# Two gated long convolutions: intermediate layouts in which PSUM copies write short contiguous runs

## The chip, the cores and the metric

The kernel runs on one core of a Trainium2 chip. The metric is the device time of one execution in microseconds (us). The engines are called as in the profile: PE (TensorE, matmuls), PEld (its weight loads), DVE (VectorE), ACT (ScalarE), POOL (GpSimd) and SP (SyncE, which here only issues DMAs).

## The reference, cut to what matters

Input x has 2048 time steps of 448 channels in bf16. Branch A is a state-space convolution: its kernel is a sum over 256 complex modes per channel. Branch B multiplies x by a convolution of a gated, shifted product of k and v with a kernel that is given. A sigmoid gate mixes the two.

```python
# A: kernel from modes, then a causal convolution of length 2048
P = exp(logdA[:, :, None] * arange(L));  K = einsum("dn,dnl,dn->dl", C, P, dB).real
a = irfft(rfft(pad(u)) * rfft(pad(K)))[:L] + u * Dskip
# B: 4-tap shift of k, product with v, causal convolution with ssm_k
kv = shift(k, shift_k) * v
b  = x * (irfft(rfft(pad(kv)) * rfft(pad(ssm_k)))[:L] + kv * ssm_D)
g  = sigmoid((x * gate_w).sum(-1, keepdims=True))
return g * a + (1 - g) * b
```

## The kernel before, in words

Time is split as 32 x 64 (a, b) and the channels as 4 groups of 112. A tile of data has the partition (group, a) and the free dimensions b (64) and channel (112). The 112 channels are worked on in two halves H of 56, each seen as 2 x 28: the pair index h and the index w (NW = 28).

Each convolution is done by transforms that are written as matmuls.

- `fft` has two stages. The first, on line L212, takes for each w one 128 x 128 block of data as the stationary operand and 256 columns (real and imaginary part r, 32 frequencies k, 4 groups g). Four such results fill one PSUM tile `ps_c` (128 x 1024, f32), and `evac` copies it to the tile `zs` in SBUF as bf16; seven copies make up one `zs`. In the second stage (L223 to L226) each of the 32 values of k takes four matmuls of 112 columns from `zs`. Four values of k fill one PSUM tile `ps_2` (2 parts of 448), which `evac` copies to `dst`, called X for data and K for a convolution kernel. Eight such copies make up one X or K.
- `products` multiplies X and K on DVE into T and, in place, X (L257, L259, L260).
- `inverse` has two stages as well. The first (L240) takes four matmuls of 256 columns for each w, four w to a PSUM tile `ps_a`, and `evac` copies it to U (seven copies). The second (L248) takes two matmuls of 56 columns for each of the 64 values of b, 16 values of b to a PSUM tile `ps_b`. DVE consumes that tile directly: `epilogue_B` (L639) multiplies it into the tile ug, and `epilogue_A` multiplies it by the gate (L646) and adds it to ug (L649).
- `KGen.block` makes an eighth of branch A's kernel. DVE builds powers of the modes in the tile `kg_T` (about 60 instructions: L294 to L332), and PE sums them in 224 small matmuls (L342) into `ps_k`, which `evac` copies to a slice of the tile S. The tile `kg_T` has one buffer, so a block can begin only when the matmuls of the one before have read it. Three small copies on ACT (L284, L285, L311) start a block. After four blocks `KGen.gather` (L377) spreads S into the tile KT.

`evac` is one line, `nc.scalar.copy(dst, src)` on L508; so all these copies stand under that line in the profile, on ACT, and are told apart by their tiles.

The program runs eight transforms and four inverses: K and X of branch B for the first half and its inverse, the same for the second half, then branch A. The eight generator blocks stand between them. The language's scheduler fixes the order of the instructions on each engine when the kernel is built, and semaphores carry the dependences, so each engine works through its own list in order. Large tiles (zs, X, K, T, U, kv, uu, ...) share a pool of five buffers, and PSUM tiles of the transforms share three.

In the layouts before the change, `zs` is [r, k, g, w], so one copy, which goes through w and then through (r, k, g), writes consecutive elements 28 elements apart. `U` is [w, h, r, b], which one copy fills in order; the second stage then reads 56 columns that lie 128 or 256 elements apart. S is [b, h, v], and the copy goes through b innermost, writing 56 elements apart. The gate's multiplication of u (L607) reads the factor `og`, one value for each b, with the step 0 along the 112 channels.

## Time and profile before

| | us |
|---|---|
| median of 3 runs | 691.45 (689.78 to 693.69) |
| profiled execution, its own time | 694.0 |
| profiled execution, its span | 692.2 |
| PE busy (PEld busy) | 285.0 (253.0) |
| DVE busy | 302.7 |
| ACT busy | 413.0 |
| POOL busy | 10.6 |

Over the span the granted TensorE clock has a mean of 0.696 of full speed. The rows of the profile show an instruction's line, engine, operation, the tile that it writes and those it reads, the shapes, the number of instructions, and busy time, mean duration and the idle time of the engine just before them with what ended it. "Chain" is the chain of work that ended last, followed back from the last instruction to whatever released each step. Line numbers are those of the kernel before, unless a row is said to be of the changed kernel, where most lines stand two or three further down.

### The profile page before, as it was taken

To read this page: it belongs to the slowest core of one execution; us is meant where nothing else is said; L and a number is where in the kernel's file an instruction comes from. 1 tells how busy PE (TensorE), PEld (TensorE's weight loads), DVE (VectorE), ACT (ScalarE), POOL (GpSimd) and SP (SyncE) were. 2 spreads that over 40 slices of the span, in tenths; PEclk is the share of its full clock that TensorE was granted. 3 is DMA by queue.
4 is the path that set the end of the run, shared out by engine and by line. 5 is a ranking of instruction groups with operands and counts; after the bars stand their busy time and mean duration, and the time that the engine had idled before them with its cause. 6 is when DMAs were issued, how large, how long until landed. Compare 5 with 4: busy or idle time off the path is not lost.

```text
span 692.2 us, 9722 instructions
## 1 busy us (share of the span) xinstructions
PE 285.0 (41%) x4272; PEld 253.0 (37%) x4272; DVE 302.7 (44%) x554; ACT 413.0 (60%) x238; POOL 10.6 (2%) x122
## 2 busy tenths in 40 slices
PE   1100123103844951216154197353126983531694
PEld 1000113102843951106153197342124971521584
DVE  5378431892297958009105975046019330000403
ACT  0556999309861440898966053990983539899340
POOL 4000000000000000000000000000000000000000
PEclk9999999655566955556567595576656955665685
DMA  9976410017101141000100181000000000000005
GB/s 186 121 112 166 110 29 1 0 25 113 59 0 47 22 80 43 4 0 1 45 2 1 46 109 39 8 2 2 0 0 1 3 1 0 1 0 1 1 1 106
DMA packets 77602, 25.74 MB, mean 37 GB/s; under 512 B 73592, under 2 KB 76536, under 8 KB 77560
## 3 DMA queue, kind: packets, MB, share of 16 engines
q1 hardware_dynamic: 59372, 20.72, 15.0%
q10 hardware_dynamic: 18188, 4.40, 4.0%
q8 instruction: 33, 0.54, 0.3%
q14 instruction: 9, 0.07, 0.0%
HBM read 17.09 MB, written 8.03 MB: 36 GB/s over the span
## 4 chain that ended last, share of the span: by engine, by line
ACT 42%; PE 27%; DVE 21%; issue 4%; ACTq 2%; POOL 1%; DMA 1%; POOLq 0%; SPq 0%
ACT zs L508 32%; PE ps_a L240 7%; PE ps_b L248 7%; DVE kg_P L294 5%; PE ps_k L342 4%; PE ps_gate L602 2%; DVE kv L590 2%; DVE T L257 2%; DVE kg_T L301 2%; DVE kg_T L302 2%; PE ps L223 1%; ACT X L508 1%; DVE kvt L589 1%; PE ps L225 1%; PE ps L224 1%
## 5 line engine op out<-in xcount | busy, mean ns | idle before, releaser
L508 ACT CAST zs<-ps_c 128x1024 bf16<-128x1024 f32 x56 | 248.0, 4831 | 53.6 <-PE ps_c L212 53.6
L294 DVE TENSOR_TENSOR kg_P<-kg_T,kg_E 128x896 bf16<-128x896 bf16 (+2 forms) x104 | 73.5, 745 | 98.2 <-ACT kg_T L285 98.2
L223 PE MATMUL ps<-zs,s_C 128*128 128x112 bf16 x256 | 61.7, 249 | 84.2 <-ACT zs L508 84.2
L508 ACT CAST S<-ps_k 128x448 bf16<-128x448 f32 x8 | 18.2, 2275 | 103.0 <-PE ps_k L342 103.0
L240 PE MATMUL ps_a<-sa_r,T 128*128 128x256 bf16 x224 | 46.3, 293 | 44.2 <-DVE T L257 30.7
L224 PEld LDWEIGHTS <-s_S 128*128 128x128 bf16 x256 | 30.4, 119 | 86.7 <-issue 86.7
L224 PE MATMUL ps<-zs,s_S 128*128 128x112 bf16 x256 | 61.8, 250 | 0.0
L225 PE MATMUL ps<-zs,s_N 128*128 128x112 bf16 x256 | 61.6, 249 | 0.0
L226 PE MATMUL ps<-zs,s_C 128*128 128x112 bf16 x256 | 61.4, 249 | 0.0
L248 PE MATMUL ps_b<-U,sb_G 128*128 128x56 bf16 x512 | 50.8, 275 | 3.9 <-ACT U L508 3.9
L248 PEld LDWEIGHTS <-sb_G 128*128 128x128 bf16 x512 | 49.9, 122 | 4.8 <-issue 4.8
L257 DVE TENSOR_TENSOR T<-X,K 128x7168 bf16<-128x7168 bf16 x4 | 15.6, 3888 | 82.3 <-ACT K L508 81.8
L508 ACT CAST U<-ps_a 128x1024 bf16<-128x1024 f32 x28 | 28.5, 1025 | 35.9 <-PE ps_a L240 35.8
L212 PE MATMUL ps_c<-Wc,sk 128*128 128x256 bf16 x56 | 12.7, 385 | 89.6 <-DVE sk L566 59.6
L240 PE MATMUL ps_a<-sa_r,X 128*128 128x256 bf16 x224 | 45.3, 288 | 3.4 <-DVE X L260 2.1
L240 PEld LDWEIGHTS <-T 128*128 128x128 bf16 x224 | 29.2, 147 | 46.1 <-DVE T L257 44.8
L212 PEld LDWEIGHTS <-sk 128*128 128x128 bf16 x56 | 7.1, 130 | 94.5 <-DVE sk L566 60.1
L342 PE MATMUL ps_k<-kg_T 128*32 128x32 bf16 x1792 | 31.1, 241 | 21.3 <-DVE kg_T L301 12.1
L342 PEld LDWEIGHTS <-kg_T 128*32 128x32 bf16 x1792 | 29.0, 148 | 23.9 <-DVE kg_T L301 12.3
L212 PE MATMUL ps_c<-Wc,kv 128*128 128x256 bf16 x56 | 12.7, 381 | 59.7 <-DVE kv L591 32.2
L307 DVE TENSOR_TENSOR kg_T<-kg_E 128x112 bf16<-128x112 bf16 x8 | 1.7, 217 | 76.1 <-PE ps_k L342 71.5
L508 ACT CAST X<-ps 128x896 bf16<-128x896 f32 x32 | 27.8, 930 | 11.0 <-PE ps L226 7.9
(139 smaller groups left out, 585.9 us busy)
## 6 DMA issues: line engine op xcount, KB each, us to landing
kg_E<-ed SPq DMA_DIRECT2D x8, 756.0 KB, 4.4
ed<-ks_E SPq DMA_DIRECT2D x11, 448.0 KB, 3.4
uu<-in_A_u_dram SPq DMA_DIRECT2D x6, 448.0 KB, 8.8
skraw<-in_B_ssm_k_dram SPq DMA_DIRECT2D x16, 112.0 KB, 4.8
ed<-ks_mag SPq DMA_DIRECT2D x5, 224.0 KB, 4.1
kt<-in_B_k_dram ACTq DMA_DIRECT2D x2, 448.0 KB, 12.8
kt<-in_B_k_dram SPq DMA_DIRECT2D x2, 448.0 KB, 12.1
vt<-in_B_v_dram ACTq DMA_DIRECT2D x2, 448.0 KB, 15.2
```

The costliest lines, as they stand in the source:

```text
L212: nc.tensor.matmul(pt[:, i, :], lhsT=cols(4 * j + i), rhs=W[:], start=True, stop=True)
L223: nc.tensor.matmul(re, lhsT=c, rhs=zr, start=True, stop=False)
L224: nc.tensor.matmul(re, lhsT=s, rhs=zi, start=False, stop=True)
L225: nc.tensor.matmul(im, lhsT=n, rhs=zr, start=True, stop=False)
L226: nc.tensor.matmul(im, lhsT=c, rhs=zi, start=False, stop=True)
L240: nc.tensor.matmul(pt[:, i, :], lhsT=lhsT, rhs=r, start=(n == 0), stop=(n == 3))
L248: nc.tensor.matmul(o, lhsT=G[:, b, r].rearrange("p g a -> p (g a)"), rhs=U[:, :, :, r, b].rearrange("p w h -> p h w"), start=(r == 0), sto ...
L257: V.tensor_tensor(out=T[:].rearrange("p r k c -> p (r k c)"), in0=X[:].rearrange("p r k c -> p (r k c)"), in1=K[:].rearrange("p r k c -> p ...
L294: V.tensor_tensor(out=P4[:, :, i * m:(i + 1) * m].rearrange("p v n c m -> p v (n c) m"), in0=T[:, lo:lo + m].rearrange("p n c m -> p (n c) ...
L301: V.tensor_tensor(out=T[:, dst:dst + n, 0], in0=P4[:, 0, 0:n, 0], in1=P4[:, 1, 0:n, 1], op=ALU.subtract)
L342: nc.tensor.matmul(pt[32 * g:32 * g + 32, hw, :].rearrange("p (i j) -> p i j", i=2), lhsT=T[:, 0:32, c, m], rhs=rhs, start=(hf == 0 and c ...
L508: nc.scalar.copy(dst, src)
```

## The change

Five layouts change, and with them the access patterns of the instructions that write or read them; the matmuls and their number stay.

- `zs` becomes [r, k, w, g]. One copy now goes through (r, k), then 4 values of w, then 4 groups, and writes 16 elements in a row; from PSUM it reads four f32 in a row and then jumps by 256. The second stage's 112 columns become (w, g).
- The copy into X or K undoes that: it reads PSUM with the step 4, and it is issued once for each of the two parts, so 128 copies of 448 elements take the place of 64 of 896. X and K keep their layout.
- `U` becomes [r, b, w, h], with the columns of the three R tables ordered (c, h) to match. One copy writes 8 elements in a row and reads two f32 in a row, then jumps by 256. The 56 columns of the last stage's matmuls are now contiguous, and the result in `ps_b` comes as (w, h); the epilogues read it with the step 2 to keep ug as it was.
- The copy into S goes through the channels innermost: it writes 7 elements in a row and reads PSUM with the step 32.
- `og` holds each value twice, and L607 is written over pairs of channels.

```diff
--- before.py
+++ after.py
@@ -129,9 +129,9 @@
         nc.scalar.activation(v[:], low16(ph[:].rearrange("p i b -> p (i b)")), ACT.Sin, scale=PHASE)
         out = []
         for nm, lo, sg in (("1", 0, 1.0), ("2", 0, -1.0), ("3", 128, 1.0)):
-            R = self.pool.tile([P, 2, 128], bf16, name="sa_r" + nm)
+            R = self.pool.tile([P, 128, 2], bf16, name="sa_r" + nm)
             for h in range(2):
-                nc.vector.tensor_scalar(out=R[:, h, :], in0=v[:, lo:lo + 128], scalar1=mask[:, h:h + 1], scalar2=sg,
+                nc.vector.tensor_scalar(out=R[:, :, h], in0=v[:, lo:lo + 128], scalar1=mask[:, h:h + 1], scalar2=sg,
                                         op0=ALU.mult, op1=ALU.mult)
             out.append(R)
         return out
@@ -204,32 +204,34 @@
 
 def fft(nc, psum, pool, W, C2, cols, dst, evac):
     C, S, N = C2
-    zs = pool.tile([P, 2, 32, 4, NW], bf16, name="zs", tag="big")
-    zw = zs[:].rearrange("p r k g w -> p w (r k g)")
+    zs = pool.tile([P, 2, 32, NW, 4], bf16, name="zs", tag="big")
+    zw = zs[:].rearrange("p r k w g -> p (r k) w g")
     for j in range(NW // 4):
         pt = psum.tile([P, 4, 256], f32, name="ps_c", tag="ps")
         for i in range(4):
             nc.tensor.matmul(pt[:, i, :], lhsT=cols(4 * j + i), rhs=W[:], start=True, stop=True)
-        evac(zw[:, 4 * j:4 * j + 4, :], pt[:])
+        evac(zw[:, :, 4 * j:4 * j + 4, :], pt[:].rearrange("p i (rk g) -> p rk i g", g=4))
     for kk in range(8):
         pt = psum.tile([P, 2, 512], f32, name="ps_2", tag="ps")
         for i in range(4):
             k = 4 * kk + i
             o = i * 112
-            zr = zs[:, 0, k].rearrange("p g w -> p (g w)")
-            zi = zs[:, 1, k].rearrange("p g w -> p (g w)")
+            zr = zs[:, 0, k].rearrange("p w g -> p (w g)")
+            zi = zs[:, 1, k].rearrange("p w g -> p (w g)")
             re, im = pt[:, 0, o:o + 112], pt[:, 1, o:o + 112]
             c, s, n = (t[:, k].rearrange("p h s -> p (h s)") for t in (C, S, N))
             nc.tensor.matmul(re, lhsT=c, rhs=zr, start=True, stop=False)
             nc.tensor.matmul(re, lhsT=s, rhs=zi, start=False, stop=True)
             nc.tensor.matmul(im, lhsT=n, rhs=zr, start=True, stop=False)
             nc.tensor.matmul(im, lhsT=c, rhs=zi, start=False, stop=True)
-        evac(dst[:, :, 4 * kk:4 * kk + 4, :].rearrange("p r k c -> p r (k c)"), pt[:, :, 0:448])
+        for r in range(2):
+            evac(dst[:, r, 4 * kk:4 * kk + 4, :].rearrange("p k (g w) -> p k g w", g=4),
+                 pt[:, r, 0:448].rearrange("p (k w g) -> p k g w", k=4, g=4))
 
 
 def inverse(nc, psum, pool, R, G, T, X, evac, consume):
-    R1, R2, R3 = (r[:].rearrange("p h c -> p (h c)") for r in R)
-    U = pool.tile([P, NW, 2, 2, 64], bf16, name="U", tag="big")
+    R1, R2, R3 = (r[:].rearrange("p c h -> p (c h)") for r in R)
+    U = pool.tile([P, 2, 64, NW, 2], bf16, name="U", tag="big")
     prods = ((T[:, 0], R1), (T[:, 1], R2), (X[:, 0], R3), (X[:, 1], R3))
     for j in range(NW // 4):
         pt = psum.tile([P, 4, 256], f32, name="ps_a", tag="ps")
@@ -238,15 +240,15 @@
             for n, (t, r) in enumerate(prods):
                 lhsT = t.rearrange("p k (g w) -> p (k g) w", w=NW)[:, :, w]
                 nc.tensor.matmul(pt[:, i, :], lhsT=lhsT, rhs=r, start=(n == 0), stop=(n == 3))
-        evac(U[:, 4 * j:4 * j + 4].rearrange("p w h r b -> p w (h r b)"), pt[:])
+        evac(U[:, :, :, 4 * j:4 * j + 4].rearrange("p r b w h -> p (r b) w h"), pt[:].rearrange("p i (rb h) -> p rb i h", h=2))
     for b0 in range(0, 64, 16):
         pt = psum.tile([P, 2, 512], f32, name="ps_b", tag="ps")
         for i in range(16):
             b = b0 + i
-            o = pt[:, i // 8, (i % 8) * 56:(i % 8) * 56 + 56].rearrange("p (h w) -> p h w", h=2)
+            o = pt[:, i // 8, (i % 8) * 56:(i % 8) * 56 + 56]
             for r in range(2):
                 nc.tensor.matmul(o, lhsT=G[:, b, r].rearrange("p g a -> p (g a)"),
-                                 rhs=U[:, :, :, r, b].rearrange("p w h -> p h w"), start=(r == 0), stop=(r == 1))
+                                 rhs=U[:, r, b].rearrange("p w h -> p (w h)"), start=(r == 0), stop=(r == 1))
         consume(b0, pt)
 
 
@@ -342,7 +344,7 @@
                         nc.tensor.matmul(pt[32 * g:32 * g + 32, hw, :].rearrange("p (i j) -> p i j", i=2),
                                          lhsT=T[:, 0:32, c, m], rhs=rhs, start=(hf == 0 and c == 0), stop=(hf == 1 and c == 1),
                                          tile_position=(0, 32 * g))
-        evac(S[:].rearrange("p b (h v) -> p h v b", h=2)[:, :, v0:v0 + CW, :], pt[:].rearrange("p (h w) b -> p h w b", h=2))
+        evac(S[:].rearrange("p b (h v) -> p b h v", h=2)[:, :, :, v0:v0 + CW], pt[:].rearrange("p (h w) b -> p b h w", h=2))
 
     def gather(self, cons, S, KT, evac):
         nc = self.nc
@@ -602,9 +604,10 @@
             nc.tensor.matmul(pg[:], lhsT=ones[:], rhs=ug[:, :, l], start=(l == 0), stop=(l == 111))
         gt = wp.tile([P, 64], f32, name="gt")
         sg = nc.scalar.activation(gt[:], pg[:], ACT.Sigmoid)
-        og = wp.tile([P, 64], bf16, name="og")
-        V.tensor_scalar(out=og[:], in0=gt[:], scalar1=-1.0, scalar2=1.0, op0=ALU.mult, op1=ALU.add)
-        V.tensor_tensor(out=ug[:], in0=uu[:], in1=og[:].unsqueeze(2).to_broadcast([P, 64, 112]), op=ALU.mult)
+        og = wp.tile([P, 64, 2], bf16, name="og")
+        V.tensor_scalar(out=og[:], in0=gt[:].unsqueeze(2).to_broadcast([P, 64, 2]), scalar1=-1.0, scalar2=1.0, op0=ALU.mult, op1=ALU.add)
+        pairs = lambda t: t[:].rearrange("p b (n t) -> p b n t", t=2)
+        V.tensor_tensor(out=pairs(ug), in0=pairs(uu), in1=og[:].unsqueeze(2).to_broadcast([P, 64, 56, 2]), op=ALU.mult)
 
         R = cons.stage_a(cons.field("sA", 0, 63), cons.onehot("mhA", 2, cons.field("hA", 6, 1)))
         G = cons.stage_b(cons.field("kB", 2, 31, 4.0, 1.0), cons.onehot("mgB", 4, cons.field("gB", 0, 3), 1.0 / 2048))
@@ -636,17 +639,17 @@
         def consume(b0, pt):
             for i in range(2):
                 o = ug[:, b0 + 8 * i:b0 + 8 * i + 8, :].rearrange("p b (h v) -> p b h v", h=2)[:, :, :, H * NW:(H + 1) * NW]
-                V.tensor_tensor(out=o, in0=pt[:, i, 0:448].rearrange("p (b h w) -> p b h w", b=8, h=2), in1=o, op=ALU.mult)
+                V.tensor_tensor(out=o, in0=pt[:, i, 0:448].rearrange("p (b w h) -> p b h w", b=8, h=2), in1=o, op=ALU.mult)
         return consume
 
     def epilogue_A(H):
         def consume(b0, pt):
-            t = kgp.tile([P, 16, 56], bf16, name="ept", tag="ept", bufs=2)
+            t = kgp.tile([P, 16, 2, NW], bf16, name="ept", tag="ept", bufs=2)
             for i in range(2):
-                V.tensor_tensor(out=t[:, 8 * i:8 * i + 8, :], in0=pt[:, i, 0:448].rearrange("p (b c) -> p b c", b=8),
-                                in1=gt[:, b0 + 8 * i:b0 + 8 * i + 8].unsqueeze(2).to_broadcast([P, 8, 56]), op=ALU.mult)
+                V.tensor_tensor(out=t[:, 8 * i:8 * i + 8], in0=pt[:, i, 0:448].rearrange("p (b w h) -> p b h w", b=8, h=2),
+                                in1=gt[:, b0 + 8 * i:b0 + 8 * i + 8].unsqueeze(2).unsqueeze(3).to_broadcast([P, 8, 2, NW]), op=ALU.mult)
             o = ug[:, b0:b0 + 16, :].rearrange("p b (h v) -> p b h v", h=2)[:, :, :, H * NW:(H + 1) * NW]
-            V.tensor_tensor(out=o, in0=t[:].rearrange("p b (h w) -> p b h w", h=2), in1=o, op=ALU.add)
+            V.tensor_tensor(out=o, in0=t[:], in1=o, op=ALU.add)
             if H == 1:
                 for g in range(4):
                     dmae[g % 2].dma_start(out4[g][:, b0:b0 + 16, :], ug[g * 32:(g + 1) * 32, b0:b0 + 16, :])
```

The scheduler keeps the order of most work. On ACT, this is the stretch from the second inverse to branch A's first kernel spectrum. U, zs, S, K are the tiles written by `evac`; the three COPY rows are those that start a generator block. Before:

```order
L508 CAST U<-ps_a 128x1024 x7
L508 CAST zs<-ps_c 128x4x256 x7
L508 CAST S<-ps_k 128x2x7x32
L284 COPY kg_T<-kg_E 128x224
L285 COPY kg_T<-kg_E 128x224
L508 CAST K<-ps_3901 128x2x448
L311 COPY kg_T<-kg_E 128x112
L508 CAST K<-ps_3919 128x2x448
```

And in the changed kernel:

```order
L510 CAST U<-ps_a 128x128x8 x7
L510 CAST zs<-ps_c 128x64x16 x7
L510 CAST S<-ps_k 128x64x7
L286 COPY kg_T<-kg_E 128x224
L287 COPY kg_T<-kg_E 128x224
L510 CAST K<-ps_3933 128x448 x2
L313 COPY kg_T<-kg_E 128x112
L510 CAST K<-ps_3952 128x448 x2
```

Nothing moved here: the shapes of the writes changed, each K copy became two, and the generator's copies still stand behind the seven zs copies.

On DVE the products of branch B's second half moved. KT is the gathered kernel of branch A, T and X are the products, and the kg rows belong to generator block 4. Before, T stood at the end of the block:

```order
L301 TENSOR_TENSOR kg_T<-kg_P_3054 128x4x112
L302 TENSOR_TENSOR kg_T<-kg_P_3054 128x4x112
L331 TENSOR_TENSOR kg_T<-kg_T 128x3584
L294 TENSOR_TENSOR kg_P_3059<-kg_T,kg_E 128x2x224
L257 TENSOR_TENSOR T<-X,K 128x7168
L301 TENSOR_TENSOR kg_T<-kg_P_3059 128x112
L302 TENSOR_TENSOR kg_T<-kg_P_3059 128x112
L259 TENSOR_TENSOR X<-X,K 128x3584
```

In the changed kernel T stands ahead of the block:

```order
L688 TENSOR_TENSOR KT<-KT,dA 128x56
L259 TENSOR_TENSOR T<-X,K 128x7168
L296 TENSOR_TENSOR kg_P_3036<-kg_T,kg_E 128x2x224
L296 TENSOR_TENSOR kg_P_3040<-kg_T,kg_E 128x2x224
L303 TENSOR_TENSOR kg_T<-kg_P_3036 128x112
L304 TENSOR_TENSOR kg_T<-kg_P_3036 128x112
```

T moved from the end of block 4 to its start, and the two products into X stayed at its end.

## The prediction

> **What bounds the kernel now.** I read the page's busy times first, then the chain of work that ended last, then the forms and times of the helper line that empties PSUM, then the stretches between the instants at which the chain changes its subject, and last the single rows whose durations the sum needs.
>
> ```profile
> PE 285.0 (41%) x4272; PEld 253.0 (37%) x4272; DVE 302.7 (44%) x554; ACT 413.0 (60%) x238; POOL 10.6 (2%) x122
> ACT 42%; PE 27%; DVE 21%; issue 4%; ACTq 2%; POOL 1%; DMA 1%; POOLq 0%; SPq 0%
> ```
>
> No engine is full, but ACT holds 42% of the chain. The helper line L508 alone is most of that; split by what it writes (min/median/max in ns):
>
> ```profile
> L508 ACT CAST zs<-ps_c x56: 4499/4849/5282, 82.6 to 634.1; 128x1024 bf16<-128x1024 f32 x56
> L508 ACT CAST K<-ps x32: 905/918/965, 116.7 to 647.3; 128x896 bf16<-128x896 f32 x32
> L508 ACT CAST X<-ps x32: 905/912/1260, 197.4 to 605.7; 128x896 bf16<-128x896 f32 x32
> L508 ACT CAST U<-ps_a x28: 1007/1012/1373, 225.0 to 669.5; 128x1024 bf16<-128x1024 f32 x28
> L508 ACT CAST KT<-ps_g x16: 532/549/875, 366.1 to 606.9; 128x448 bf16<-128x448 f32 x16
> L508 ACT CAST S<-ps_k x8: 2207/2244/2547, 222.2 to 547.2; 128x448 bf16<-128x448 f32 x8
> L564 ACT COPY sk<-skraw x2: 4170/4182/4193, 77.0 to 254.3; 128x3584 bf16<-128x3584 bf16 x2
> L578 ACT COPY wt<-wraw 128x448 bf16<-128x448 bf16 x1 | 0.6, 592 | 0.0
> ```
>
> zs and U have the same number of elements and the same kind of source, yet zs takes 4.8 times as long. KT (448 elements) and X (896) give the price of a plain copy: (912 - 549) / 448 = 0.81 ns an element and 186 ns fixed; U fits it (186 + 1024 x 0.81 = 1015). Taking off the 186 ns, zs costs 4.55 ns an element and S 4.59. Both read PSUM in order; what they have in common is the write: consecutive elements land 56 bytes apart in zs and 112 bytes apart in S. sk writes 4 bytes apart and costs 1.115 ns an element, so four of them 4.46 ns. The three rows agree on some 4.5 ns for each 16 bytes of SBUF that a copy touches (an estimate from these rows), which hides behind 8 x 0.81 = 6.5 ns when the 16 bytes are filled. A strided read in SBUF is cheap: wt reads 8 bytes apart at 592 ns against KT's 549.
>
> Where the time lies, by stretches (start, end and length in us, then busy us and number of instructions of PE, its weight loads, DVE, ACT and POOL, TensorE's granted clock, DMA share and GB/s):
>
> ```profile
> 82.60:124.10 41.50, 14.67 (x152) 12.02 (x150) 10.13 (x11) 39.92 (x17) 2.16 (x2) 1.00 0.08 23
> 124.10:197.30 73.20, 23.19 (x172) 20.91 (x173) 46.08 (x34) 36.45 (x15) 0.00 (x0) 0.52 0.25 47
> 197.30:282.10 84.80, 44.55 (x1023) 42.36 (x1021) 64.71 (x141) 25.61 (x26) 0.00 (x0) 0.70 0.18 40
> 282.10:425.20 143.10, 65.84 (x1045) 58.66 (x1045) 62.84 (x140) 91.89 (x57) 0.00 (x0) 0.63 0.14 25
> 425.20:564.10 138.90, 69.02 (x1234) 61.71 (x1232) 53.85 (x113) 90.74 (x48) 0.00 (x0) 0.65 0.02 7
> 564.10:692.20 128.10, 61.46 (x600) 52.02 (x598) 17.03 (x19) 84.72 (x43) 0.00 (x0) 0.62 0.08 15
> ```
>
> ACT is nearly full in the first stretch and busy for two thirds of the last three. DVE, which would be next, is starved by it: the copies that a block of the kernel generator needs (L284, L285, L311) stand behind the seven zs copies in ACT's queue.
>
> ```profile
> DVE kg_P L294 <- ACT kg_T L285: 98.2, 8, 33.0
> ```
>
> **The change, part by part.**
>
> *zs and S.* zs now gets runs of 16 elements (32 bytes, two filled 16-byte pieces): by the rows above 186 + 1024 x 0.81 = 1.02 us, some 0.95 from start to start. S gets runs of 7 elements (14 bytes), which mostly straddle two pieces: 64 runs x 9 ns + 186 = 0.76 us for 2.24. Bounds for zs: 1.0 us (the U row) and 4.8 (no gain); I take the low end because the write pattern is then like U's. On the way in, both now read PSUM with jumps (four f32 in a row, then 1 KB on; for S single f32 128 bytes apart), which no row shows on ACT.
>
> *K and X.* One copy of 896 becomes two of 448 that read single f32 16 bytes apart and write in order. At KT's 549 ns, and 0.97 for two (first row below), a pair costs 0.97 for 0.91, so a transform's eight pairs take 7.5 to 7.8 us, as now, where TensorE's second stage is about as long. If the read is slow it costs more; the nearest strided reads of f32 words have no row, so I bound it below by 0.81 ns an element and above by the write price, 4.5. I take 0.81, by the wt row.
>
> *U.* Runs of 8 elements, 16 bytes: 1.01 us, or 1.34 if each straddles. The second row below shows the cover: the copy waits 0.73 us for TensorE each time. Beyond 1.75 us that cover is gone.
>
> ```profile
> 366.13 0.97 ACT L508 CAST KT<-ps_g 128x448 bf16<-128x448 f32 x2
> 667.72 1.01 ACT L508 CAST U<-ps_a 128x1024 bf16<-128x1024 f32 x1 [0.73 <-PE ps_a L240]
> 551.44 12.66 PE ps_b L248 x128
> 643.09 0.21 PE L226 MATMUL ps<-zs,s_C 128*128 128x112 bf16 x1
> 643.14 0.21 PE L223 MATMUL ps<-zs,s_C 128*128 128x112 bf16 x1
> 175.63 13.46 PE ps_gate L602 x112
> ```
>
> *The last stage's matmuls.* 128 of them in 12.66 us are 99 ns each for 56 columns that lie 512 bytes apart; in the second stage 112 columns in a row go every 49 ns (643.09, 643.14). The gate's matmuls, 64 columns 224 bytes apart, need 120. So a strided column costs about 1.8 ns, and the change makes these columns lie in a row: at most 49 ns each, 6.3 us for an inverse, so 6.3 saved in each of four (between 0 and 9.5). The weight load might hold it above 49; I take 49 since that row loads as many weights.
>
> *Epilogues.* L639 and L646 read PSUM 8 bytes apart. At today's price two of them (1.16 us for 16 b) stay under TensorE's 32 x 49 ns = 1.57; in epilogue A, with L649, they take 1.75 and set the pace.
>
> ```profile
> L639 DVE TENSOR_TENSOR ug<-ps_b,ug 128x448 bf16<-128x448 f32 x16 | 9.2, 619 | 5.1 <-PE ps_b L248 5.0
> L597 DVE TENSOR_TENSOR ug<-uu,gw x1: 3892/3892/3892, 166.0 to 166.0; 128x7168 bf16<-128x7168 bf16 x1
> L607 DVE TENSOR_TENSOR ug<-uu,og x1: 7626/7626/7626, 189.7 to 189.7; 128x7168 bf16<-128x7168 bf16 x1
> ```
>
> *L607* takes twice L597's time on the same sizes; its third operand repeats one element, the new one repeats a pair. I take 3.9 us (bounds 3.9 and 7.6); it is on the chain. The R tables' strided writes are six instructions of 0.25 us in setup, behind other work.
>
> *Order.* DVE now does the second product T before block 4 rather than after it. Its 3.8 us and the block's 17.9 (372.06 to 389.93 below) are serial in both, and TensorE needs both before going on, so this costs nothing or a microsecond.
>
> **The sum**, stretch by stretch, with seven zs copies as 6.5 to 7.5 us where they took 31. These rows of the chain (start, length) and one of the waits carry the rest:
>
> ```profile
> 154.16 2.04 DVE kv L591
> 372.06 0.69 DVE kg_P L294 x2
> 389.93 3.81 DVE T L257
> 399.19 12.28 PE ps_a L240 x111
> 478.13 3.60 PE ps_k L342 x188
> 485.37 30.59 ACT zs L508 x7
> 525.37 3.89 DVE T L257
> 629.81 9.17 ACT zs L508 x2
> 648.32 3.90 DVE T L257
> 670.53 12.66 PE ps_b L248 x128
> 684.94 0.63 DVE ug L649
> DVE ug L597 <- DMA uu<-in_A_u_dram: 9.8, 1, 9.8
> ```
>
> A second stage with its copies takes 9.3 us now (last zs ends at 638.98, T starts at 648.32).
> - 82.6 to 124.1: 7 zs + 2 + 2 for the two sine activations between them + 9 for K: 18.5 after 41.5, -23. The end is when K's last matmul frees zs for kvt.
> - 124.1 to 197.3: the DVE chain for kv (32, 124.1 to 156.2), the load of u (9.8 after it), L597 (3.9), the gate (13.5), sigmoid and og (0.6), L607 (3.9): 63.8, -9.4. The zs copies hide under it; the gate before waited for them.
> - 197.3 to 282.1: blocks 0 to 2 of the generator, bound by DVE and by the single kg_T buffer, stay (each 18 us, with 3.6 us of matmuls and up). Saved are L248's 6.3, of which block 1 takes some back, and 1.5 for each S on the way: -6.1.
> - 282.1 to 425.2: zs 6.5, K 9.5, zs 6.5, X and its gathers 18, T 3.9, block 4 18.1, X products 4, ps_k 5, ps_a 12.3, U 1, ps_b 6.3: 91, -52. Block 3 hides under the transforms (18 us under 30).
> - 425.2 to 564.1: here DVE comes next. Rest of block 5 and its matmuls behind the zs copies 11.5, S and copies 1.5, block 6 18.2, ps_k 5, S 1, zs 7.5, X 9.3, then T to the end of ps_b 32.4 (525.37 to 564.10, 38.7, less 6.3): 86.4, -52.5.
> - 564.1 to the end: zs and KT 9, X 9.3, KT 1.2, zs 8, K 9.5, from T to the last stage 22.2 (648.32 to 670.53), ps_b with the epilogues 8.6, output 6.6 (685.57 to the end) to 8.6, since the output leaves in a shorter time: 75.5, -52.5.
>
> Together -195.5: a span of 497 us for 692.2. The profiled execution took 694.0, 1.8 more than its span and 0.4% above the median of 691.45. With those 1.8 and a few microseconds for what I could not place, I predict 502.
>
> **A page that speaks against it.** The Trainium skill, Advanced Engine Details and Errata, section Memory Cachelines, gives PSUM lines of 8 bytes, two f32, and wants every two consecutive elements to be contiguous. By that rule the K, X and S copies and the epilogues, which now take one f32 per line, would read slowly while zs and U (four and two in a row) would not; the page gives no price, and no row of this trace shows ACT on such a read. What it would make of the time is the first rival.
>
> **Rivals.**
> - *Single f32 reads from PSUM are slow.* The only strided reader with a price is TensorE, 99/56 = 1.77 ns a column. With that, a K or X copy takes 186 + 448 x 1.77 = 0.98 us, a pair 1.8 for 0.95, 6.8 us more in each transform. Two of the eight are covered (by blocks 0 and 6), so +41, and +6 for the epilogues: 549. For it: TensorE's price. Against: wt's 8%.
> - *The write gains less than the runs suggest* (zs at 2 to 2.8 us): about 45 of 56 copies lie on the path, so +45 to +80: 545 to 580. For it: no row shows runs of 32 bytes. Against: the three rows that fit one price for 16 bytes.
> - *Slower than before.* If single f32 reads cost what single writes do, 4.5 ns, then 128 copies and 32 epilogue instructions of 448 elements pay 3.7 ns more on 71,680 elements, +265, and the kernel takes about 760. The point from which it decides: 195 us / 71,680 = 2.7 ns more, that is 3.5 ns an element. Nothing in the trace reads that slowly: TensorE pays half of it.
> - *Nothing is freed, since another engine binds.* DVE has 303 us of work, ACT would have about 220, PE 285 by a busy time that overlaps. None reaches 497, and the stretches above already carry DVE's blocks; so at most the middle stretches lose 10 us or so each, inside the range.
>
> **How the numbers follow.** Plain reads and full write gain: 0.58, 480 to 520. Slow single reads: 0.24, 520 to 580. Smaller write gain: 0.12, 530 to 600. Slower or same: 0.04. Quicker than 480, TensorE staying at the full clock: 0.02. The range from 482 to 568 leaves out the tails of these, under 0.2. Half a per cent is about what a measurement of this kernel can tell from no change; the cases give faster 0.96, same 0.01, slower 0.03.
>
> **What would show it.** zs copies near 1.0 us and S near 0.8; K and X copies at 0.55 (slow reads: 0.9 or more); U at 1.0 and still waiting for TensorE; L248 every 49 ns; L607 at 3.9; DVE's wait for L285 down from 98 us to under 30, and DVE's generator blocks a larger share of the chain than ACT's zs. The prediction is wrong if K and X exceed 0.8 us, if zs exceeds 1.5, or if TensorE goes through the second stage's 128 matmuls slower than ACT's 7.7 us, over 60 ns each, and sets that stage instead.

## The result, and the profile after

The changed kernel takes 486.9 us (median of four runs, 484.0 to 487.8) where the kernel before took 691.6 beside it (689.8 to 693.7): a ratio of 0.703, with a 95% interval of 0.700 to 0.707. The prediction said 502, with 482 to 568 as its range. The profiled execution took 484.0, with a span of 482.2.

From the page of the changed kernel, the busy times and the chain that ended last (which the profile followed back only to 206.8 us, so its shares do not fill the span):

```profile
PE 228.9 (47%) x4272; PEld 204.3 (42%) x4272; DVE 298.3 (62%) x554; ACT 210.1 (44%) x302; POOL 10.6 (2%) x122
DVE 26%; PE 14%; ACT 12%; issue 3%; ACTq 0%
```

ACT lost 203 us of work and DVE 4, and DVE now leads the chain. The helper line that empties PSUM (L510 now, L508 before), by what it writes (min/median/max in ns):

```profile
L510 ACT CAST K<-ps x64: 530/599/712, 91.6 to 443.6; 128x448 bf16<-128x448 f32 x64
L510 ACT CAST X<-ps x64: 532/568/662, 161.8 to 426.0; 128x448 bf16<-128x448 f32 x64
L510 ACT CAST zs<-ps_c x56: 987/1042/1280, 81.8 to 433.7; 128x1024 bf16<-128x1024 f32 x56
L510 ACT CAST U<-ps_a x28: 1012/1012/1017, 189.7 to 465.0; 128x1024 bf16<-128x1024 f32 x28
L510 ACT CAST KT<-ps_g x16: 538/587/687, 271.7 to 426.8; 128x448 bf16<-128x448 f32 x16
L510 ACT CAST S<-ps_k x8: 577/645/661, 187.1 to 400.8; 128x448 bf16<-128x448 f32 x8
```

zs fell from 4849 to 1042 ns and S from 2244 to 645. K and X read PSUM 16 bytes apart, S reads it 128 bytes apart, and none of them is far from KT, which reads in order.

The six stretches of the prediction, cut at the same events (columns as there: start, end and length in us, then busy us of PE, PEld, DVE, ACT and POOL with their instructions, granted clock, DMA share, GB/s):

```profile
81.84:97.96 16.12, 13.26 (x152) 10.97 (x150) 10.12 (x10) 15.59 (x24) 2.16 (x2) 1.00 0.21 58
97.96:161.76 63.80, 22.09 (x171) 20.50 (x172) 42.39 (x34) 12.27 (x17) 0.00 (x0) 0.54 0.29 54
161.76:241.30 79.54, 37.31 (x1018) 35.02 (x1017) 64.69 (x142) 21.82 (x34) 0.00 (x0) 0.67 0.19 43
241.30:326.00 84.70, 49.78 (x1052) 43.52 (x1050) 61.45 (x138) 41.01 (x72) 0.00 (x0) 0.83 0.23 42
326.00:408.90 82.90, 54.99 (x1232) 49.35 (x1232) 53.21 (x114) 38.56 (x64) 0.00 (x0) 0.81 0.04 11
408.90:482.20 73.30, 45.03 (x600) 39.73 (x600) 18.21 (x22) 37.17 (x59) 0.00 (x0) 0.81 0.15 26
```

The lengths were 41.5, 73.2, 84.8, 143.1, 138.9 and 128.1 before. DVE's busy time in the third to fifth stretch is what it was (64.7, 61.5, 53.2 against 64.7, 62.8, 53.9): the same work stands closer together. Its wait for ACT at the head of a generator block, 98.2 us before, from the table of waits (total, times, longest):

```profile
DVE kg_P L296 <- ACT kg_T L287: 19.7, 7, 7.6
```

### The profile page after: what moved, and what is told of

It is laid out like the page before. It is cut to its first block, busy times and chain, and to the rows that moved or that the text cites. A ratio compares the mean times of both kernels' runs of the same rounds, so it can differ in the third digit from the quotient of the medians.

```text
span 482.2 us, 9795 instructions
## 1 busy us (share of the span) xinstructions
PE 228.9 (47%) x4272; PEld 204.3 (42%) x4272; DVE 298.3 (62%) x554; ACT 210.1 (44%) x302; POOL 10.6 (2%) x122
## 4 chain that ended last, share of the span: by engine, by line
DVE 26%; PE 14%; ACT 12%; issue 3%; ACTq 0%
DVE kg_P L296 9%; PE ps_k L344 6%; PE ps_a L242 5%; ACT zs L510 5%; ACT X L510 3%; DVE kg_T L303 3%; DVE kg_T L304 3%; DVE T L259 2%; DVE kg_T L333 2%; ACT K L510 1%; DVE X L261 1%; DVE ept L649 1%; DVE ug L642 1%; DVE kg_T L311 1%; ACT KT L510 1%
## 5 line engine op out<-in xcount | busy, mean ns | idle before, releaser
L510 ACT CAST zs<-ps_c 128x1024 bf16<-128x1024 f32 x56 | 52.6, 1065 | 37.1 <-PE ps_c L212 36.9
L223 PE MATMUL ps<-zs,s_C 128*128 128x112 bf16 x256 | 55.8, 229 | 13.5 <-ACT zs L510 13.5
L242 PE MATMUL ps_a<-sa_r,T 128*128 128x256 bf16 x224 | 46.3, 296 | 29.1 <-DVE T L259 16.3
L224 PE MATMUL ps<-zs,s_S 128*128 128x112 bf16 x256 | 55.9, 230 | 0.0
L242 PE MATMUL ps_a<-sa_r,X 128*128 128x256 bf16 x224 | 45.6, 290 | 21.6 <-DVE X L261 19.5
L225 PE MATMUL ps<-zs,s_N 128*128 128x112 bf16 x256 | 55.8, 230 | 0.0
L226 PE MATMUL ps<-zs,s_C 128*128 128x112 bf16 x256 | 55.7, 229 | 0.0
L510 ACT CAST S<-ps_k 128x448 bf16<-128x448 f32 x8 | 5.0, 631 | 107.6 <-PE ps_k L344 107.6
L510 ACT CAST U<-ps_a 128x1024 bf16<-128x1024 f32 x28 | 28.4, 1013 | 39.8 <-PE ps_a L242 28.6
L242 PEld LDWEIGHTS <-X 128*128 128x128 bf16 x224 | 29.1, 146 | 24.9 <-DVE X L261 20.9
L224 PEld LDWEIGHTS <-s_S 128*128 128x128 bf16 x256 | 27.5, 107 | 15.9 <-issue 15.7
L510 ACT CAST X<-ps 128x448 bf16<-128x448 f32 x64 | 29.5, 578 | 7.7 <-PE ps L226 4.8
L303 DVE TENSOR_TENSOR kg_T<-kg_P 128x448 bf16<-128x448 bf16 (+2 forms) x104 | 31.9, 306 | 0.1
L304 DVE TENSOR_TENSOR kg_T<-kg_P 128x448 bf16<-128x448 bf16 (+2 forms) x104 | 31.9, 306 | 0.0
L510 ACT CAST K<-ps 128x448 bf16<-128x448 f32 x64 | 28.6, 601 | 3.1 <-PE ps L226 3.1
```

The lines of the kernel that those rows point to most:

```text
L223: nc.tensor.matmul(re, lhsT=c, rhs=zr, start=True, stop=False)
L224: nc.tensor.matmul(re, lhsT=s, rhs=zi, start=False, stop=True)
L225: nc.tensor.matmul(im, lhsT=n, rhs=zr, start=True, stop=False)
L226: nc.tensor.matmul(im, lhsT=c, rhs=zi, start=False, stop=True)
L242: nc.tensor.matmul(pt[:, i, :], lhsT=lhsT, rhs=r, start=(n == 0), stop=(n == 3))
L303: V.tensor_tensor(out=T[:, dst:dst + n, 0], in0=P4[:, 0, 0:n, 0], in1=P4[:, 1, 0:n, 1], op=ALU.subtract)
```

## Experiments: which part of the change did it

Theory W is the prediction's: the scattered write made ACT slow, and its cure is nearly all. The rivals give the gain to the last stage's contiguous columns (C) or to the parts acting only together (D). The edits below are shortened: a tile followed by a pattern in quotes stands for its rearranged view, and `...` for what stays.

**zs alone, on the kernel before.**

```
-    zs = pool.tile([P, 2, 32, 4, NW], ...)
+    zs = pool.tile([P, 2, 32, NW, 4], ...)      # with its copies, its reader, and K/X split in two
```

> The kernel before with the new layout of zs alone (and the split K and X copies that go with it); U, the last stage, S, og and the epilogues as before. Theory W (the scattered write made ACT slow, and its cure is nearly the whole gain): zs copies at 1.04 us; what is missing against the changed kernel's 487 us is four times 6 to 8 us for the last stage's matmuls at 99 ns, up to 8 us for S and 3.7 us for the product with og, so 520 to 532 us, point 527. Rival C (the contiguous columns of the last stage carry much of the gain): 560 us or more. Rival D (the parts only work together, since another slow part takes the place of zs on the path): 600 us or more.

Measured: 522.1 us (520.9 to 523.4), ratio 0.753 [0.751, 0.755]. Of the 205 us, 171 come with zs alone. W holds; C and D fall.

**All but zs.**

> The changed kernel with the layout of zs and the K and X copies as before; U, the last stage, S, og and the epilogues stay changed. Theory W: zs copies at 4.85 us again, ACT again the engine that ends most waits; the other edits give what the first run lacks, at most 40 us and less where ACT hides them: 650 to 670 us, point 658. Rival C: below 630 us. Rival D: 680 to 692 us.

Measured: 652.3 us, ratio 0.941 [0.939, 0.943]; zs back at 4834 ns a copy. 171 and 41 make 212, a little more than the 205 that the two bring together, so neither needs the other.

**The inverse alone.**

> The kernel before with the inverse alone changed: R tables, U, the last stage's matmuls and the epilogues; zs, S and og as before. The last stage's matmuls go from 99 to 27 ns each, and DVE's epilogues set its pace; theory W: 4 times 6 to 7 us less where nothing covers it, 664 to 674 us, point 668. If ACT's late copies take the gain back (the next transform's zs copies are what the path waits for anyway): 680 to 690. Rival C: below 650.

Measured: 668.1 us, ratio 0.964 [0.961, 0.966], 25 us less than the kernel before. The group of the last stage's matmuls in this run's trace (busy us, mean ns of one that overlaps its neighbours), which in the run with zs alone, where U keeps its old layout, is 50.8, 275:

```profile
L248 PE MATMUL ps_b<-U,sb_G 128*128 128x56 bf16 x512 | 15.6, 192 | 6.7 <-ACT U L508 3.9 <-DVE ug L639 2.8
```

**S undone, on the changed kernel.**

```
-evac(S "p b (h v) -> p b h v"[..., v0:v0+CW], pt "p (h w) b -> p b h w")
+evac(S "p b (h v) -> p h v b"[:, :, v0:v0+CW], pt "p (h w) b -> p h w b")
```

> The changed kernel with the copy of S as before (single elements 112 bytes apart): 2.23 us for 0.645, eight times. The two runs that left out zs and all but the inverse differ by 15.8 us, of which og is 3.7, so S would be worth up to 12; in the changed kernel the copies that start the generator's next block stand behind S on ACT and DVE waits for them. If nearly every S counts: 495 to 500 us, point 497. If DVE's waits for ACT are shorter than before and hide it: 488 to 492.

Measured: 497.2 us (496.5 to 499.9), 10.3 above the changed kernel, with S at 2.22 us. Eight copies lost 1.58 us each, 12.6 in all, so most of it counts; a block's first copies stand behind S in ACT's queue.

## Experiments: what makes a write dear

**Only the order of writing.** The prediction priced a write by the 16-byte pieces that it touches. This run leaves every layout as before and only turns the copy's loop round, so that four neighbours in w are written together:

```
-zw = zs "p r k g w -> p w (r k g)";  evac(zw[:, 4*j:4*j+4, :], pt)
+zw = zs "p r k g w -> p (r k g) w";  evac(zw[:, :, 4*j:4*j+4], pt "p i c -> p c i")
```

> The kernel before with one edit: the zs copies go through the same elements in another order, so that the four neighbours in w are written one after the other (8 bytes, then a step to the next 56 bytes) and PSUM is read as single f32 1 KB apart. Layouts, K and X copies and matmuls all as before. Price by 16-byte pieces: 256 pieces of 4.5 ns and 186 ns, zs at 1.34 us, 0.3 us more than in the changed layout for each of 56 copies of which some 40 count: 535 to 548 us, point 541. Rival L (the price goes by the layout, since the same addresses are written): zs stays near 4.8 us and the time at 690. Rival R (PSUM reads 1 KB apart are slow): zs between 2 and 4 us, 580 to 650 us.

Measured: 515.5 us (512.1 to 518.1), ratio 0.743 [0.739, 0.748]: faster than the new layout alone, and faster than expected. The group of zs in its trace:

```profile
L508 ACT CAST zs<-ps_c 128x1024 bf16<-128x1024 f32 x56 | 53.0, 1056 | 54.0 <-PE ps_c L212 54.0
```

zs at 1056 ns with runs of 8 bytes is the price of runs of 32 bytes. All three theories written down for it missed: the 16-byte pieces (1.34), the layout (4.8), a slow read 1 KB apart (2 to 4). A read of single f32 1 KB apart costs nothing that shows, and the price by pieces needs a condition.

**Eight write patterns in one trace.**

```
off, order = per call of fft:   (0, pairs) (1, fours) (2, fours) (0, singles 14 B) (1, pairs) (0, singles 4 B) (0, singles 224 B) (0, singles 56 B)
zf = pool.tile([P, 7168 + 8], ...);  zs = zf[:, off:off + 7168] in before's layout
```

> The kernel before, in which each of the eight transforms writes its zs copies in another order or at another offset of the same buffer, so that one trace prices eight write patterns of 1024 elements (in the order of the calls): pairs of neighbours (4 bytes); runs of four moved by 2 bytes; runs of four moved by 4 bytes; single elements 14 bytes apart; pairs moved by 2 bytes; single elements 4 bytes apart in groups of four; single elements 224 bytes apart; single elements 56 bytes apart as before. The time of the whole means nothing here. Theory of 16-byte pieces (the prediction's, already short of the runs of four, 1.06 us where it gave 1.34): 2.5; 1.9; 1.9; 4.3 to 4.8; 3.0; 2.5; 4.8; 4.8 us. Theory N4 (only a write that leaves part of an aligned 4-byte word untouched is dear, 4.5 ns each): 1.05; 2.5; 1.05; 4.8; 4.8; 4.8; 4.8; 4.8. Theory N8 (the same with 8-byte words): 2.5; 2.5; 2.5; 4.8; 2.5 to 3.7; 4.8; 4.8; 4.8. Theory B (the step of 56 bytes is what is slow, as when successive writes meet in one bank): singles at 4, 14 and 224 bytes differ from 4.8 us by a factor.

Groups of this trace, each from the window of one transform, in the order of the list (the sixth has one run of four among its seven):

```profile
L532 ACT CAST zs_pair<-ps_c 128x1024 bf16<-128x1024 f32 x7 | 6.8, 1062 | 0.0
L532 ACT CAST zs_quad_off<-ps_c 128x1024 bf16<-128x1024 f32 x6 | 10.2, 1882 | 26.0 <-PE ps_c L226 26.0
L532 ACT CAST zs_quad_off<-ps_c 128x1024 bf16<-128x1024 f32 x7 | 7.0, 1109 | 0.0
L532 ACT CAST zs_single<-ps_c 128x1024 bf16<-128x1024 f32 x7 | 28.1, 4466 | 0.0
L532 ACT CAST zs_pair_off<-ps_c 128x1024 bf16<-128x1024 f32 x7 | 20.1, 3221 | 13.6 <-PE ps_c L226 13.6
L532 ACT CAST zs_single<-ps_c 128x1024 bf16<-128x1024 f32 x7 | 11.0, 1761 | 0.0
L532 ACT CAST zs_single<-ps_c 128x1024 bf16<-128x1024 f32 x7 | 32.7, 5064 | 12.8 <-PE ps_c L226 12.8
L532 ACT CAST zs_single<-ps_c 128x1024 bf16<-128x1024 f32 x7 | 30.7, 4792 | 0.8 <-PE ps_c L226 0.8
```

No theory got all eight. N4 is right that aligned pairs are free (1.06) and that fours moved by 4 bytes are (1.11), which the 16-byte theory priced at 2.5 and 1.9. The 16-byte theory is right on fours moved by 2 bytes (1.88) and close on pairs moved by 2 (3.22), where N4 said 2.5 and 4.8. N8 gave 2.5 for the aligned pairs, and theory B's step of 56 bytes is no special one, since 14 and 224 cost about the same; 4 bytes is cheaper, but there several singles fall into one piece. Put together: *a 16-byte piece visited with at least one 4-byte word only partly written costs 4.55 ns; whole words cost nothing beyond 0.81 ns an element, at the distances tried here (up to 224 bytes).* Counting such pieces in the order of writing (a count made after the run; the expectation's 2.5 for singles 4 bytes apart was a miscount of the same rule) and taking 186 ns plus the greater of 0.81 ns an element and 4.55 ns a piece:

| pattern | pieces with a part-written word | rule, us | measured |
|---|---|---|---|
| aligned pairs | 0 | 1.02 | 1.06 |
| fours moved by 2 bytes | 384 | 1.93 | 1.88 |
| fours moved by 4 bytes | 0 | 1.02 | 1.11 |
| singles 14 bytes apart | 896 | 4.26 | 4.47 |
| pairs moved by 2 bytes | 640 | 3.10 | 3.22 |
| singles 4 bytes apart (mean with one plain copy) | 384 | 1.80 | 1.76 |
| singles 224 and 56 bytes apart | 1024 | 4.85 | 5.06, 4.79 |
| S as changed (448) | 64 | 0.55 | 0.58 to 0.66 |
| sk as before (3584) | 896 | 4.26 | 4.18 |

The rule was fitted to three of these rows (zs and sk before, and the plain price); the others are as it gives them within 9%, but for S, up to 0.1 us above. Its condition on part-written words was read off these same patterns, so they do not test it; the one forecast made by it afterwards, for sk (below), was missed. Why the part-written word is dear was not measured. The Trainium skill (SBUF — State Buffer, Specifications (TRN2)) asks for two accesses to each 16-byte line. Aligned pairs agree with it; the moved pairs, three quarters of which also put two elements into one line and yet take three times as long, do not, so the measurement decides for the 4-byte word.

## Experiments: the columns, the order and what is left

**Steps between the last stage's columns.**

```
-U = pool.tile([P, 2, 64, NW, 2], ...)                 # columns 2 bytes apart
+U = pool.tile([P, 64 // q, NW, 2, 2, q], ...)         # q = 4, 1, 2, 64: 16, 4, 8, 256 bytes
```

> The changed kernel with four different layouts of U, one for each inverse, so that the 56 columns that a matmul of the last stage reads lie 16, 4, 8 and 256 bytes apart (in the order of the inverses), where the changed kernel has them 2 bytes apart (27 ns a matmul) and the kernel before 128 to 512 bytes apart (99 ns). The copies of U are split into eight each here, so the time of the whole means nothing. If the rate goes by whether the columns are contiguous: 99 ns for all four. If it goes by the bytes fetched in some larger unit: 4 bytes near 27 to 35, 8 bytes 40 to 55, 16 bytes and more near 99.

From windows around the four inverses (columns: length, busy us of the 128 ps_b matmuls, granted clock, DMA share, GB/s; the 16-byte one holds short waits):

```profile
190.00:260.00 70.00, 13.38 (x128) 0.68 0.18 37
340.00:360.00 20.00, 5.14 (x128) 0.71 0.07 17
425.00:440.00 15.00, 6.93 (x128) 0.89 0.01 3
490.00:512.00 22.00, 12.65 (x128) 0.69 0.26 50
```

128 matmuls at 16, 4, 8 and 256 bytes are 105, 40, 54 and 99 ns each; in the changed kernel, 2 bytes apart, 27. They did not run at the same granted clock, though. Two half microseconds of the 4-byte inverse, two of the 8-byte one (with the matmuls of which some part falls into them, then the granted clock), and two stretches of the changed kernel at 2 bytes:

```profile
349.50:350.00 0.50, 0.50 (x16) 0.50 0.00 0
352.00:352.50 0.50, 0.50 (x26) 1.00 0.00 0
433.00:433.50 0.50, 0.50 (x14) 1.00 0.00 0
435.50:436.00 0.50, 0.50 (x14) 0.50 0.00 0
213.92:215.60 1.68, 1.67 (x32) 0.50 0.14 25
466.11:469.58 3.47, 3.47 (x128) 1.00 0.02 5
```

At 2 bytes a matmul takes 27 ns at the clock 1.00 and 52 at 0.50. At 4 bytes the number also goes with the clock, 26 against 16 in half a microsecond, so the 40 ns is a mean over two clocks and no sign that 4 bytes are dearer than 2. At 8 bytes it is 14 at either clock, and at 16 bytes 12 in a microsecond at 0.50 and 13 at 1.00 (203 to 204 and 217 to 218). "Contiguous or not" falls: by these rows 2 and 4 bytes cost the same, 8 bytes twice that at the full clock and 16 twice that again, where the price stands.

**The order-only zs in the changed kernel.**

> The changed kernel, with zs and the K and X copies of the run that changed only the order of writing: layout of zs as before, runs of four (8 bytes), one copy of 896 elements for a pair of K or X. If the new layout of zs is worth nothing beyond the order: the same distance as between the two runs alone (515 against 522), so 478 to 485 us, point 480. If the longer runs and the shorter column steps of the layout matter once the rest is quicker: 487 us or more.

Measured: 480.2 us (478.8 to 481.2), ratio 0.694 [0.691, 0.696]. The new layout of zs was not needed; it even costs some 7 us, which the next run tries to place. In this run's trace T stands behind block 4 again (the block starts at 277.24, T at 295.01).

**Block 4 before the product T.** In the changed kernel DVE takes T ahead of block 4; here it is ordered behind the block, as it stood before.

```
+    if kg is not None:
+        after(kg.tc, first, kg.last)      # T behind the block's last instruction on DVE
```

> The changed kernel with the second product T put behind block 4 of the generator on DVE, as it stood before the change, and nothing else moved by hand. In the changed kernel's trace DVE idles 6.6 us until X is there, does T in 3.9 and only then starts the block; the prediction called that nothing or a microsecond. If it is what the order-only version gains: 482.5 to 484.5 us, point 483.5. If the gain of the order-only version lies in the 64 copies of K and X that it saves: 486 to 488.

DVE's rows, first of the changed kernel, then of this run:

```profile
279.10 3.89 DVE L259 TENSOR_TENSOR T<-X,K 128x7168 bf16<-128x7168 bf16 x1 [6.63 <-ACT X L510]
282.91 0.69 DVE L296 TENSOR_TENSOR kg_P<-kg_T,kg_E 128x448 bf16<-128x448 bf16 x2
309.17 0.69 DVE L296 TENSOR_TENSOR kg_P<-kg_T,kg_E 128x448 bf16<-128x448 bf16 x2 [0.93 <-ACT kg_T L287]
```

```profile
280.33 0.69 DVE L298 TENSOR_TENSOR kg_P<-kg_T,kg_E 128x448 bf16<-128x448 bf16 x2 [6.89 <-ACT kg_T L289]
298.49 3.88 DVE L259 TENSOR_TENSOR T<-X,K 128x7168 bf16<-128x7168 bf16 x1
306.34 0.69 DVE L298 TENSOR_TENSOR kg_P<-kg_T,kg_E 128x448 bf16<-128x448 bf16 x2
```

Measured: 482.3 us (481.6 to 485.0), ratio 0.698 [0.695, 0.700], 4.6 below the changed kernel by the medians; the profiled executions differ by 2.0 (480.2 against 482.2). Block 4 starts 2.6 us earlier (280.33 against 282.91), the generator's matmuls then run beside T and the X products, and block 5 starts 2.8 us earlier. So T's place costs some 2 to 5 us, part or most of the 7. The intervals of this run and of the changed kernel just touch, so even that is hardly clear of noise; what the rest is, the 64 more copies of K and X among the candidates, is not settled.

**kvt out of the large buffers.** The trace of the changed kernel shows DVE waiting 9.6 us for the load of u, which waits for a buffer that kvt holds.

```
-t = bigt([P, 32, 112], "kvt")
+t = tmp.tile([P, 32, 112], bf16, name="kvt", tag="t8", bufs=2)
```

> The changed kernel with one edit: kvt (the product that the short convolution adds up) lies in the pool of setup instead of taking one of the five large buffers, so that the load of u need not wait for its last use. In the changed kernel DVE waits 9.6 us for that load. If that wait is on the path: 476 to 479 us, point 477. Rival: the gate's matmuls and the generator's first block then wait for something else (the first load of the generator's exponentials, which stands behind u in its queue), and only part comes through: 480 to 486 us.

The first kvt, the issue of u's load and L599, of the changed kernel and then of this run:

```profile
97.96 2.02 DVE L591 TENSOR_TENSOR kvt<-kt,wt 128x3584 bf16<-128x3584 bf16 x1 [3.49 <-PE ps L226]
125.96 3.00 SPq L597 DMA_DIRECT2D uu<-in_A_u_dram  x2
139.68 3.89 DVE L599 TENSOR_TENSOR ug<-uu,gw 128x7168 bf16<-128x7168 bf16 x1 [9.62 <-DMA uu<-in_A_u_dram]
```

```profile
83.21 2.02 DVE L591 TENSOR_TENSOR kvt<-kt,wt 128x3584 bf16<-128x3584 bf16 x1
98.82 2.95 SPq L597 DMA_DIRECT2D uu<-in_A_u_dram  x2
116.87 3.88 DVE L599 TENSOR_TENSOR ug<-uu,gw 128x7168 bf16<-128x7168 bf16 x1
```

Measured: 470.7 us (469.5 to 471.1), ratio 0.680 [0.678, 0.682], 16.3 less and more than the wait that I had counted. kvt had also taken zs's buffer and so waited for the first transform to end (97.96); without that, the sum for kv begins some 15 us earlier and ends at 115.6 instead of 130.1. L599 starts 22.8 us earlier; where the other 6.5 are lost was not followed.

**All of it, and sk in the order of its writing.**

```
-nc.scalar.copy(sk "p v b h -> p v h b", rawk)
+nc.scalar.copy(sk, rawk "p v h b -> p v b h")
```

> The order-only version of the changed kernel (480 us), with kvt in the setup's pool (16 us less on the changed kernel), and with the sk copy in the order of its writing, so that each 4-byte word is written whole: by the rule that only part-written words are dear, 4.18 us becomes 2.9 to 3.1 (3584 elements at 0.75 to 0.81 ns), twice, of which one or both count. Sum 462 to 464.5 us, point 463. If sk's price is its strided access and not the part-written words, sk stays near 4.2 us and the time at 464 to 466.

Measured: 462.5 us (460.8 to 462.9), ratio 0.668 [0.666, 0.670]: the fastest version of all, and where the sum put it.

```profile
L564 ACT COPY sk<-skraw x2: 3566/3568/3570, 76.6 to 198.4; 128x3584 bf16<-128x3584 bf16 x2
```

sk fell from 4.18 to 3.57, between the two theories: it now writes whole words but reads SBUF 128 bytes apart, at (3568 - 186) / 3584 = 0.94 ns an element, near the 0.91 of wt's strided read ((592 - 186) / 448, with the 186 ns of the copies from PSUM). The strided read as the cause of what is left is argued, not shown: this run does not separate the two.

**The gate's columns in a row.**

```
-V.tensor_tensor(out=ug, in0=uu, in1=gw over b);              rhs=ug[:, :, l]
+V.tensor_tensor(out=ugt, in0=uu "p b l -> p l b", in1=gw...); rhs=ugt[:, l, :]
```

> The version before this one, with the gate's product written with b innermost, so that the 64 columns of each of the gate's 112 matmuls lie in a row. By the price of columns (99 ns for 56 columns 16 bytes apart and more, 27 ns in a row) the gate's matmuls take 3.5 to 4.5 us for 13.6; DVE's product then reads bf16 224 bytes apart, which no row shows; bounds 3.9 us (plain) and 7.6 (the old og product, which also repeated one element). At 7.6: 6 us less on the path, 457 us, range 454 to 460. If the strided read on DVE costs 14 us or more, nothing is won: 462 to 468.

Measured: 466.0 us (462.6 to 467.8), ratio 0.673 [0.670, 0.675]; no gain. Both sides of the trade, from the groups of this trace:

```profile
L598 DVE TENSOR_TENSOR ug<-uu,gw 128x7168 bf16<-128x7168 bf16 x1 | 13.6, 13577 | 0.0
L603 PE MATMUL ps_gate<-ug,ones 128*128 128x64 bf16 x112 | 5.4, 228 | 3.2 <-DVE ug L598 3.2
```

The matmuls fell from 13.6 to 5.4 us. The 27 ns for 56 columns would make that 3.5 us at the full clock (an estimate); these ran at a granted clock of 0.60 (130.21 to 135.59), at which it would be 5.8. But DVE's product rose from 3.9 to 13.6: 1.89 ns an element where one operand is read 224 bytes apart and the other repeats an element, beyond my upper bound of 7.6, so the second case written down, that nothing is won, is the one that came. Which share the distance has and which the repeating was not separated.

## Why the prediction was right, and where its terms were off

- *zs writes* (the step that carries the sum): right in place and in size, 1.04 us for 1.02 predicted. The reason given was incomplete. The price by 16-byte pieces is true only of pieces with a part-written word; filling the pieces was not needed, and aligned pairs would have done.
- *S*: predicted 0.76, measured 0.645. The 9 ns a run for straddling were far too much: by their place in the row the copies took 0.58, 0.65, 0.65 and 0.63 us (187.10, 214.02, 240.55 and 270.34), at most 1.6 ns a run above the plain 0.55. A run of seven leaves one word part-written, which by the rule hides behind its elements. Undoing S cost 10.3 us.
- *K and X*: taken at the plain price, measured 0.60 and 0.57 for KT's 0.587. The rival of slow single f32 reads, at 0.24, did not occur, nor did the one that ended slower: ACT reads PSUM 16 bytes, 128 bytes and 1 KB apart without a price, and DVE 8 bytes apart (612 ns for 619). The Trainium skill's rule on 8-byte lines in PSUM (Advanced Engine Details and Errata, Memory Cachelines) is not borne out for reads by these two engines.
- *Last stage*: mis-sized. I took 49 ns a matmul, since a row with as many weights had that; it is 27, at the low end that I had named. That row's 49 ns were its 112 columns, 0.44 ns each at a granted clock of 1.00, and not its weights: 27 ns for 56 columns are 0.48 each with as many weights, also at 1.00. With 3.47 us a stage, DVE's epilogues set the pace. That the inverse alone brings 25 us, as four times 6.3 said, is partly luck: TensorE saves 9.2 us an inverse, and the epilogues let only a part of it through (in the third inverse, from the first matmul to the end of the last epilogue, 15.1 us before and 7.6 with the inverse alone). The stage and one epilogue of the changed kernel:

```profile
466.11 3.47 PE L250 MATMUL ps_b<-U,sb_G 128*128 128x56 bf16 x128 [1.10 <-ACT U L510]
L649 DVE TENSOR_TENSOR ept<-ps_b,gt x16: 608/612/625, 406.1 to 472.5; 128x448 bf16<-128x448 f32 x16
```

- *The second stage*: one sign by which I would have been wrong came halfway. Its 128 matmuls took 7.9 to 8.1 us in four of the eight transforms, 62 to 63 ns each, over the 60 that I had named. From the last transform, ACT's copies, then two microseconds of TensorE with the matmuls in them and the granted clock:

```profile
436.55 0.97 ACT L510 CAST K<-ps 128x448 bf16<-128x448 f32 x2 [1.74 <-PE ps L226]
438.04 6.21 ACT L510 CAST K<-ps 128x448 bf16<-128x448 f32 x14 [0.53 <-PE ps L226]
434.86:435.86 1.00, 1.00 (x12) 0.50 0.00 0
439.86:440.86 1.00, 1.00 (x25) 1.00 0.00 0
```

TensorE goes through the first three microseconds at half the pace, in which ACT waits for it twice; from then on ACT's last 14 copies run without a wait. So TensorE sets the start of the stage and ACT the rest, and the stage with its copies took the 9.5 us that I had put down (from 434.8 to 444.3). In three of the four the granted clock of the slow microseconds is 0.50, as here; in the first transform the profile gives 1.00 for the same slow start, so the clock is not shown to be the cause there.
- *L607 (L610 now)*: 3.9 us as predicted, and the second stretch is 63.8 us to the digit.
- *Order*: "nothing or a microsecond" was too little; T ahead of block 4 costs some 2 to 5, as far as two intervals that touch can tell.
- *The sum*: the stretches came out at 16.1, 63.8, 79.5, 84.7, 82.9 and 73.3 for 18.5, 63.8, 78.7, 91, 86.4 and 75.5. The span is 14.3 us below the 497 of the sum, of which 6.3 lie in the fourth stretch: K and X with their copies took 7.8 and 16.8 us there for the 9.5 and 18 that I had put down, the X products and the generator's matmuls (ps_k) 7.2 together where I had them one after the other at 9, and ps_b 5.2 for 6.3. The rest is two to three and a half microseconds in each of three more stretches, and the few microseconds set aside for what I could not place were not needed. The terms written down for the first stretch (6.5 to 7.5, 2, 2 and 9) add up to 19.5 or more and not to 18.5; it came out shorter still, since K took 6.3 us behind the second sine (91.62 to 97.96) where I had 9.

## What to carry to other kernels

When a copy on ScalarE writes bf16, look at the order in which it writes before changing a layout: two neighbours written together, on a 4-byte boundary, are enough, and the strided read from PSUM that this takes is free. For TensorE bring the moving columns to within 4 bytes of each other, but count who pays for the transposition. And once the bound has moved, look for buffers that are held: the edit of one line on kvt brought more than all the last stage's matmuls could still give.

## What the runs showed that I had not expected

- ScalarE's write price depends on whether 4-byte words are written whole: 1.06 us for pairs 56 bytes apart on the boundary, 3.22 for the same pairs moved by 2 bytes.
- TensorE's price of a column steps with the distance, and only the dense columns go with the granted clock: 56 columns 2 bytes apart take 27 ns at 1.00 and 52 at 0.50, 4 bytes apart no more by the rows above, 8 bytes apart 54 at either clock, 16 and 256 bytes apart 105 and 99.
- VectorE takes 13.6 us for a bf16 product with one operand read 224 bytes apart and the other repeating an element, and 3.9 for the same product with u read in order.
